# Loading the first tokens' keys and queries in fp32 and reordering the opening of a window-attention and SwiGLU kernel

## The chip, the cores and the metric

The kernel runs on one core of a Trainium2 chip. The metric is device time in microseconds: 252.29 us, the median of three runs (251.28 to 253.04) of the kernel before. The profiled execution took 250.18 us, of which the trace spans 247.8 us. TensorE ran at its full granted clock throughout.

## The reference

The kernel computes attention with a sliding window of 128 tokens plus four "sink" tokens, for 4 sequences of 768 tokens and 8 heads of 64, and feeds the result, seen as 3072 tokens of 512, to a gated feed-forward layer with 1536 hidden units.

```python
scores = scale * np.matmul(q, k.transpose(0, 1, 3, 2))
keep = is_sink | in_window            # key < 4, or 0 <= query - key < 128
scores = np.where(keep, scores, -1e9)
a = np.exp(scores - max); a = a / (sum(a) + 1e-9)
x = (a @ v).transpose(0, 2, 1, 3).reshape(B * S, H * D)
g = x @ w_gate
out = (g * sigmoid(g) * (x @ w_val)) @ w_out
```

## The kernel before

Tokens are handled in 12 groups of 256, three to a sequence. For a group, keys and queries are transposed (`step_T`), multiplied (`step_S`, followed by an exp on ScalarE and a 0/1 mask on VectorE), combined with the values (`step_PV`, followed by a normalisation on VectorE that gives `xn`), and the result is transposed to `xT` (`step_X`). `step_K` does the scores of the four sink keys, which groups after the first of a sequence need apart. The feed-forward part works on blocks of 256 or 512 tokens: `gate` units (gate product `pg`, tanh `th`, value product `pv`, then `u` and `ht` on VectorE), and `down` products. Blocks 0, 1 and 2 are groups 0, 1 and 2. Each engine runs its own instructions in the order in which they are written; the order is laid out by hand.

```python
# loads of the opening: half of group 0's heads by the hardware queues in fp32, half by GpSimd as bf16
for i, eng in ((0, nc.sync), (1, nc.scalar)):
    st = stp.tile([P, 4, 2 * D], FP32, tag="st", name="st")
    eng.dma_start(st, by_two((k, q)[i], 0))
    first.append(st)
nc.scalar.activation(warmed, one, AF.Exp)
nc.gpsimd.dma_start(x0[:, 0, 4:8], by_two(k, 4))
# ... iota tq, iota tk (for identity and masks)
nc.gpsimd.dma_start(x0[:, 1, 4:8], by_two(q, 4))
load_rows(1); load_v(0); load_gate(0); load_v(1)
# ... iota th8 (for the sink table), load_gate(1..3), load_rows(2), load_v(2), load_gate(4), load_out(0..3)
```

```python
def gate(tb, f, attn):
    # ...
    pg = project(wgs, "pg")
    th = tpool.tile([P, 512], FP32, tag="th", name="th")
    nc.scalar.activation(th, pg, AF.Tanh, scale=0.5)
    for a in attn:
        a()                                   # attention steps woven into this unit
    pv = project(wvs, "pv")
    u = upool.tile([P, 512], BF16, tag="u", name="u")
    nc.vector.scalar_tensor_tensor(u, th, 1.0, pg, op0=ALU.add, op1=ALU.mult)
    nc.vector.tensor_tensor(hts[tb][:, f:f + two]..., u, pv, op=ALU.mult)
    flush()                                   # VectorE work put off by the attention steps
```

```python
# the opening
fill(8, ...)                                  # dummy matmuls
for p in range(2):                            # pairs of heads
    nc.vector.tensor_copy(out=x0[:, 0, h], in_=first[0][:, h])
    nc.scalar.copy(out=x0[:, 1, h], in_=first[1][:, h])
    pair_T(p, "a")                            # transposes; key copied by ScalarE, query by VectorE
pair_S(0, 1)                                  # scores and exp of a pair; 1: one dummy matmul first
pair_T(2, "v")
pair_S(1)
pair_mask(0)
pair_T(3, "v"); pair_S(2, 1); pair_mask(1); pair_S(3, 1); pair_mask(2)
step_T(1, 0, 0, "a"); pair_mask(3); step_T(1, 1, 0, "v"); step_T(1, 0, 1, "a"); step_T(1, 1, 1, "v")
step_S(1, 0)                                  # its masks are put off as masks1
step_PV(0, 0, 0); step_PV(0, 0, 1); flush()
step_PV(0, 1, 0); step_PV(0, 1, 1); step_X(0, 0); flush()
step_S(1, 1); step_X(0, 1)
# ... xT of group 0, tables lt8 and diag_h, step_ks(0) (kss and vsb), then the four masks1
us = [g0[0], (alone, 0, 0), g0[1], g1[0], g1[1],
      g0[2], g1[2], g0[3], g1[3], g0[4], g1[4], g0[5], g1[5],
      *g2, *downs(0), *downs(1), *downs(2)]
weave(us, slots((0, [K(1)]), (1, PVs(1) + Xs(1)),
                ((5, 5, 6, 6), T(2)), ((7, 8), Ss(2)), (8, [K(2)]), ...))
```

Of the kernel before, what the change touches and what calls it, by code (L numbers as in the profile page):

```python
# [14 lines left out]
def kernel(  # L15
# [12 lines left out]
    nc = tc.nc  # L28
# [31 lines left out]
    wpool = pool("wpool", 1)  # L60
    rowp = pool("rowp", 3)
    natp = pool("natp", 3)
    stp = pool("stp", 2)
    vpool = pool("vpool", 1)
    kqtp = pool("kqtp", 2)
    epool = pool("epool", 2)
# [101 lines left out]
    def by_two(src, h0):  # L168
        return src[0, h0:h0 + 4, 0:256].rearrange("h (m r) d -> m h (r d)", r=2)

    x0 = const.tile([P, 2, H, 2 * D], BF16)
    first = []
    for i, eng in ((0, nc.sync), (1, nc.scalar)):
        st = stp.tile([P, 4, 2 * D], FP32, tag="st", name="st")
        eng.dma_start(st, by_two((k, q)[i], 0))
        first.append(st)
    nc.scalar.activation(warmed, one, AF.Exp)

    nc.gpsimd.dma_start(x0[:, 0, 4:8], by_two(k, 4))
    nc.gpsimd.iota(tq, [[1, P]], base=0, channel_multiplier=0,  # L180
                   allow_small_or_imprecise_dtypes=True)
    nc.gpsimd.iota(tk, [[0, 1]], base=0, channel_multiplier=1,
                   allow_small_or_imprecise_dtypes=True)
    nc.gpsimd.dma_start(x0[:, 1, 4:8], by_two(q, 4))
    load_rows(1)
    load_v(0)
    load_gate(0)
    load_v(1)
    nc.gpsimd.iota(th8, [[-32, NP2], [-NS, 2]], base=0, channel_multiplier=1,
                   allow_small_or_imprecise_dtypes=True)  # L190
    load_gate(1)
    load_gate(2)
    load_gate(3)
# [63 lines left out]
    def step_ks(b):  # L257
        for h in range(2):
            r = slice(h * D, (h + 1) * D)
            nc.vector.tensor_copy(  # L260
                out=kss[r, b, :, h * NS:(h + 1) * NS], in_=kTs[b][r, :, 0:NS])
        vsb = const.tile([P, H, D + 1], BF16, tag=f"vsb{b}", name="vsb")
        nc.vector.tensor_tensor(  # L263
            vsb,
            vcf[:, b:b + 1].broadcast_to([P, H, D + 1]),
            diag_h.rearrange("q (h o) -> q h o", o=1).broadcast_to([P, H, D + 1]),
            op=ALU.mult)
        vsbs.append(vsb)
# [74 lines left out]
    def dense(t, c, n):  # L343
        return t[:, 0:c * n].rearrange("p (c n) -> p c n", c=c)

    def step_X(g, j):
        t0 = g * 256 + j * P
        tb = max(i for i in range(len(SIZES)) if OFF[i] <= t0)
        off = t0 - OFF[tb]
        if off == 0:  # L350
            xTs[tb] = dense(xtp.tile([P, DMC * 512], BF16, tag="xT", name="xT"),
                            DMC, SIZES[tb])
        if g >= XB:
            def sp():
                nc.sync.dma_start_transpose(xTs[tb][:, :, off:off + P], xns[g, j])
            later.append(sp)
            return
        pt = bank([P, DMC, P], BF16, "px")
        for i in range(DMC):
            nc.tensor.transpose(pt[:, i], xns[g, j][:, i * P:(i + 1) * P], ident)  # L360

        def dve():
            nc.vector.tensor_copy(out=xTs[tb][:, :, off:off + P], in_=pt)  # L363
        later.append(dve)
# [109 lines left out]
    def pair_T(p, key_eng):  # L474
        new_T(0)
        pt = bank([P, 2, 256], FP32, "pt")
        for i in range(2):
            for r in range(2):
                for w in range(2):
                    nc.tensor.matmul(  # L480
                        pt[64 * w:64 * (w + 1), i, r:256:2],
                        x0[:, i, 2 * p + w, r * D:(r + 1) * D], ident,
                        start=True, stop=True, skip_group_check=True)
        if key_eng == "a":
            nc.scalar.copy(out=kTs[0][:, p, 0:256], in_=pt[:, 0])
        else:
            nc.vector.tensor_copy(out=kTs[0][:, p, 0:256], in_=pt[:, 0])
        nc.vector.tensor_copy(out=qTs[0][:, p, 0:256], in_=pt[:, 1])

    def pair_S(p, n=0):  # L490
        if p == 0:
            e_t[0] = epool.tile([P, H, 512], BF16, tag="e", name="e")
        pss = [bank([P, 512], FP32, "s") for _ in range(2)]
        fill(n, pss[0])
        for kk, n, col in ((0, 256, P), (P, P, 3 * P)):
            for h in range(2):
                r = slice(h * D, (h + 1) * D)
                nc.tensor.matmul(
                    pss[h][:, col:col + n], kTs[0][r, p, kk:kk + P],
                    qTs[0][r, p, kk:kk + n], start=True, stop=True)  # L500
        for h in range(2):
            nc.scalar.activation(
                e_t[0][:, 2 * p + h, P:512], pss[h][:, P:512], AF.Exp, scale=scale)

    def pair_mask(p):
        e = e_t[0][:, 2 * p:2 * p + 2, P:512]
        m = mask0.rearrange("q (o a) x -> q o (a x)", o=1)[:, :, P:512]
        nc.vector.tensor_tensor(e, e, m.broadcast_to([P, 2, 384]), op=ALU.mult)

    fill(8, bank([P, 512], FP32, "w"))  # L510
    for p in range(2):
        h = slice(2 * p, 2 * p + 2)
        nc.vector.tensor_copy(out=x0[:, 0, h], in_=first[0][:, h])
        nc.scalar.copy(out=x0[:, 1, h], in_=first[1][:, h])
        pair_T(p, "a")
    pair_S(0, 1)
    pair_T(2, "v")
    pair_S(1)
    pair_mask(0)
    pair_T(3, "v")  # L520
    pair_S(2, 1)
    pair_mask(1)
    pair_S(3, 1)
    pair_mask(2)
    step_T(1, 0, 0, "a")
    pair_mask(3)
    step_T(1, 1, 0, "v")
    step_T(1, 0, 1, "a")
    step_T(1, 1, 1, "v")
    step_S(1, 0)  # L530
    masks1 = list(later)
    later.clear()
    step_PV(0, 0, 0)
    step_PV(0, 0, 1)
    flush()
    step_PV(0, 1, 0)
    step_PV(0, 1, 1)
    step_X(0, 0)
    flush()
    step_S(1, 1)  # L540
    step_X(0, 1)
    masks1 += later[:2]
    del later[:2]
    flush()

    nc.vector.tensor_scalar(lt8, th8, float(NS), None, op0=ALU.is_lt)
    nc.vector.scalar_tensor_tensor(diag_h, th8, 0.0, lt8, op0=ALU.is_ge, op1=ALU.mult)
    step_ks(0)
    for m in masks1:
        m()  # L550
    load_rows(3)
    load_v(3)

    g0, g1, g2 = gates(0), gates(1), gates(2)
    us = [g0[0], (alone, 0, 0), g0[1], g1[0], g1[1],
          g0[2], g1[2], g0[3], g1[3], g0[4], g1[4], g0[5], g1[5],
          *g2, *downs(0), *downs(1), *downs(2)]

    def L(*fs):
        def f():  # L560
            for x in fs:
# [1 line left out]
        return f  # L563

    weave(us, slots(
        (0, [K(1)]), (1, PVs(1) + Xs(1)),
        ((5, 5, 6, 6), T(2)), ((7, 8), Ss(2)), (8, [K(2)]),
        ((9, 9, 10, 10), PVs(2)), (11, Xs(2)),
        (12, [L(A(load_nat, 4), A(load_v, 4), A(load_nat, 5), A(load_v, 5),
                A(load_nat, 6), A(load_v, 6))]),  # L570
        ((13, 14, 15, 16), T(3)), ((17, 18), Ss(3)), (18, [A(step_ks, 1)]),
        (15, [A(xbar, 4)]), (18, [A(xbar, 5)]),
        ((19, 19, 20, 20), PVs(3)), (21, Xs(3)),
        ((20, 21), Ss(4)), (21, [K(4)]),
        ((22, 22, 23, 23), PVs(4)), (23, Xs(4))))

    def pair(ga, gb, sh=0):
        s = sh
# [5 lines left out]

    weave(gates(3) + downs(3), slots(
        (0, [L(A(load_nat, 7), A(load_v, 7))]), (1, [A(xbar, 6)]),
        (2, [L(A(load_nat, 8), A(load_v, 8))]), (5, [A(step_ks, 2)]), *pair(5, 6),
        (6, [A(xbar, 7)]), (7, [L(A(load_nat, 9), A(load_v, 9))]),
        (15, [A(xbar, 8)]), (15, [L(A(load_nat, 10), A(load_v, 10))])))
    weave(gates(4) + downs(4), slots(  # L590
        *pair(7, 8), (3, [A(xbar, 9)]), (9, [A(step_ks, 3)]),
        (3, [L(A(load_nat, 11), A(load_v, 11))]), (15, [A(xbar, 10)])))
    weave(gates(5) + downs(5), slots(*pair(9, 10), (6, [A(xbar, 11)])))
    us = gates(6) + gates(7) + downs(6) + downs(7)
# [38 lines left out]
```

The softmax here doesn't subtract the row's maximum and nothing guards it: scores larger than these inputs give would overflow.

## Time and profile before

| what | value |
|---|---|
| time, median of 3 runs | 252.29 us |
| span of the trace | 247.8 us |
| TensorE matmul busy | 236.3 us (95%) |
| VectorE busy | 165.2 us (67%) |
| ScalarE busy | 109.4 us (44%) |
| moved by DMA | 27.35 MB, mean 110 GB/s |
| chain that ended last | PE 85%, DVE 10%, ACT 3%, issue 1% |

In the profile PE is TensorE's matmuls and PEld its weight loads, DVE is VectorE, ACT is ScalarE, POOL is GpSimd and SP is SyncE. A timeline row gives the start in us, the duration in us, engine, source line, operation, what is written from what, and how many instructions were merged into the row; in brackets stands the idle time before it and what ended it. A row of the waits gives who waited for whom, the total in us, how often, and the longest. In the slices each digit is a fortieth of the span, in tenths of busy time. Short names in the rows: `e` are the exponentials, `xn` the normalised attention result, `px` its transpose in PSUM, `pt` transposed keys or queries in PSUM, `x` the bf16 keys and queries of group 0.

### The profile page before, as it was taken

The numbers are of one execution on the slowest core, as the hardware profiler recorded it, in microseconds if no ns is written. First come the engines' busy times: TensorE is split into PE (matmuls) and PEld (weight loads), VectorE is DVE, ScalarE is ACT, GpSimd is POOL, SyncE is SP. The second block draws the span as 40 slices with busy tenths as digits, with TensorE's granted clock in tenths as the row PEclk, the third lists the DMA queues.
The fourth block names the chain that finished last, engine by engine and source line by source line (L and its number), as shares of the span: only waits on it lengthen the run. The fifth ranks groups of instructions, "written<-read, shape, count | busy, mean of one in ns | idle before, by whom it ended". The sixth has DMA issues, their size and how long they took to land.

```text
span 247.8 us, 5063 instructions
## 1 busy us (share of the span) xinstructions
PE 236.3 (95%) x2007; PEld 135.9 (55%) x2007; DVE 165.2 (67%) x347; ACT 109.4 (44%) x213; POOL 69.3 (28%) x91
## 2 busy tenths in 40 slices
PE   7885999999999999999999999999999999999994
PEld 2554887787655445444445455445454445478443
DVE  5799669877965189993198993198981289887100
ACT  3780348133655383631474721465611662333112
POOL 8965824993672008070043000000000000000000
PEclk9999999999999999999999999999999999999999
DMA  8999999999999759997569802551103200100132
GB/s 140 161 185 196 190 206 199 158 152 128 156 181 189 172 128 86 134 120 104 152 122 139 58 15 67 154 140 24 42 3 115 97 0 3 42 3 0 42 127 85
DMA packets 100390, 27.35 MB, mean 110 GB/s; under 512 B 86416, under 2 KB 97424, under 8 KB 100368
## 3 DMA queue, kind: packets, MB, share of 16 engines
q0 software_dynamic: 69440, 13.90, 74.7%
q1 hardware_dynamic: 30400, 12.89, 22.5%
q8 instruction: 15, 0.25, 0.4%
q10 hardware_dynamic: 528, 0.26, 0.4%
q14 instruction: 7, 0.06, 0.1%
HBM read 28.34 MB, written 6.29 MB: 140 GB/s over the span
## 4 chain that ended last, share of the span: by engine, by line
PE 85%; DVE 10%; ACT 3%; issue 1%; DVEq 0%
PE pd L414 25%; PE pv L383 24%; PE pg L383 22%; PE o L331 4%; PE s L285 4%; DVE ht L397 3%; DVE xn L337 2%; PE pt L239 2%; DVE e L297 1%; PE w L471 1%; ACT e L292 1%; DVE u L396 1%; PE pt L480 1%; PE px L360 1%; DVE vsb L263 1%
## 5 line engine op out<-in xcount | busy, mean ns | idle before, releaser
L390 ACT ACTIVATE th<-pg 128x512 f32<-128x512 f32 x72 | 43.5, 604 | 75.4 <-PE pg L383 73.3
L383 PE MATMUL pv<-xT,wv 128*128 128x256 bf16 (+1 forms) x384 | 74.3, 326 | 0.7 <-DVE ht L397 0.7
L383 PE MATMUL pg<-xT,wg 128*128 128x256 bf16 (+1 forms) x384 | 74.2, 326 | 0.6 <-DVE xT L363 0.5
L396 DVE SCALAR_TENSOR_TENSOR u<-th,pg 128x512 bf16<-128x512 f32 x72 | 49.2, 683 | 34.6 <-ACT th L390 34.3
L414 PE MATMUL pd<-wo,ht 128*128 128x512 bf16 (+1 forms) x300 | 66.0, 371 | 0.0
L397 DVE TENSOR_TENSOR ht<-u,pv 128x512 bf16<-128x512 bf16 x72 | 49.5, 688 | 10.7 <-PE pv L383 4.5
L383 PEld LDWEIGHTS <-wg 128*128 128x128 bf16 x384 | 37.5, 98 | 25.9 <-issue 0.6
L383 PEld LDWEIGHTS <-wv 128*128 128x128 bf16 x384 | 34.2, 97 | 20.7 <-issue 2.5
L292 ACT ACTIVATE e<-s 128x512 bf16<-128x512 f32 (+1 forms) x88 | 42.9, 581 | 3.6 <-PE s L285 3.5
L414 PEld LDWEIGHTS <-ht 128*128 128x128 bf16 x300 | 28.0, 98 | 28.6 <-issue 0.3
L418 ACT ACTIVATE ot<-pd 128x512 f32<-128x512 f32 (+1 forms) x25 | 14.6, 583 | 50.9 <-PE pd L414 50.9
L297 DVE TENSOR_TENSOR e<-e,mask 128x1024 bf16<-128x1024 bf16 (+1 forms) x44 | 26.8, 649 | 2.9 <-ACT e L292 2.9
L111 POOL DMA_DIRECT2D nat<-in_k_dram x16 | 14.1, 898 | 44.7 <-DMA qT<-nat 33.7
L122 POOL DMA_DIRECT2D va<-in_v_dram x24 | 21.5, 916 | 7.0 <-DMA nat<-in_q_dram 3.5
L337 DVE TENSOR_TENSOR xn<-o,rcp 128x256 bf16<-128x256 f32 x48 | 20.4, 425 | 1.7
L331 PEld LDWEIGHTS <-e 128*128 128x128 bf16 x352 | 16.6, 98 | 6.8 <-DVE e L297 0.6
L331 PE MATMUL o<-va,e 128*128 128x65 bf16 x352 | 18.2, 193 | 0.4 <-DVE e L297 0.3
L111 POOL DMA_DIRECT2D nat<-in_q_dram x16 | 14.3, 910 | 2.4 <-DMA nat<-in_k_dram 2.4
L336 DVE RECIPROCAL rcp<-o 128x4 f32<-128x4 f32 x48 | 8.5, 177 | 7.1 <-PE o L331 7.0
L285 PE MATMUL s<-qT,kT 64*128 64x128 bf16 (+1 forms) x240 | 12.9, 237 | 0.2 <-DVE qT L246 0.2
L285 PEld LDWEIGHTS <-kT 64*128 64x128 bf16 x240 | 7.8, 94 | 7.2 <-issue 6.6
L331 PE MATMUL o<-vsb,es 128*128 128x260 bf16 x32 | 8.8, 274 | 0.3 <-ACT es L311 0.3
(57 smaller groups left out, 92.2 us busy)
## 6 DMA issues: line engine op xcount, KB each, us to landing
out_dram<-ot SPq DMA_DIRECT2D x23, 256.0 KB
va<-in_v_dram POOLq DMA_DIRECT2D x24, 128.0 KB, 7.7
nat<-in_k_dram POOLq DMA_DIRECT2D x16, 128.0 KB, 6.6
nat<-in_q_dram POOLq DMA_DIRECT2D x16, 128.0 KB, 7.8
wo<-in_moe_w_out_dram POOLq DMA_DIRECT2D x4, 384.0 KB, 11.9
wg<-in_moe_w_gate_dram POOLq DMA_DIRECT2D x4, 256.0 KB, 8.2
wv<-in_moe_w_val_dram POOLq DMA_DIRECT2D x4, 256.0 KB, 8.8
rows<-in_k_dram POOLq DMA_DIRECT2D x6, 128.0 KB, 9.1
```

The lines of the kernel that those rows point to most:

```text
L111: nc.gpsimd.dma_start(x[:, i, j].rearrange("p (h d) -> p h d", d=D), src[b, :, t0:t0 + P].rearrange("h p d -> p h d"))
L122: nc.gpsimd.dma_start(va[:, j, :, 0:D], v[b, :, t0:t0 + P].rearrange("h p d -> p h d"))
L285: nc.tensor.matmul(pss[2 * pp + h][:, col:col + n], kTs[b][r, p, kk:kk + P], qTs[b][r, p, qq:qq + n], start=True, stop=True)
L292: nc.scalar.activation(e_t[g][:, h0 + h, lo:512], pss[2 * pp + h][:, lo:512], AF.Exp, scale=scale)
L297: nc.vector.tensor_tensor(e, e, m[:, :, lo:512].broadcast_to([P, 2, 512 - lo]), op=ALU.mult)
L331: nc.tensor.matmul(o, l, r, start=(i == 0), stop=(i == len(mms) - 1), skip_group_check=True)
L337: nc.vector.tensor_tensor(xns[g, j][:, 256 * hh:256 * (hh + 1)].rearrange("p (h d) -> p h d", h=4), po[:, :, 0:D], rcp.broadcast_to([P, 4, ...
L383: nc.tensor.matmul(ps[:, i * n:(i + 1) * n], ws[fi][:, c, fo * P:(fo + 1) * P], x[:, c], start=(c == 0), stop=(c == DMC - 1))
L390: nc.scalar.activation(th, pg, AF.Tanh, scale=0.5)
L396: nc.vector.scalar_tensor_tensor(u, th, 1.0, pg, op0=ALU.add, op1=ALU.mult)
L397: nc.vector.tensor_tensor(hts[tb][:, f:f + two].rearrange("p a n -> p (a n)"), u, pv, op=ALU.mult)
L414: nc.tensor.matmul(po, hts[tb][:, f, ts * P:(ts + 1) * P], wos[f // n][:, f % n, lo:hi], start=(f == 0), stop=(f == DFC - 1))
```

## The change

All of group 0's keys and queries now come in fp32 by the hardware queues of SyncE and ScalarE, in four pieces, and are cast to bf16 by VectorE (keys) and ScalarE (queries); GpSimd is left free to issue the loads of group 1 at once. The casts stand ahead of the transposes that need them, the small tables for the sink keys are made early, and the dummy matmuls between the scores are gone. ScalarE takes over the query transposes of group 1 and the `xT` copies of group 1. The transposes of group 1 are split around the value products of group 0. The value products of group 1 stood together after the first gate unit; they are now in two parts with a gate unit between them, and a third gate unit of block 0 holds the `xT` step of group 1. The aim is that TensorE has gate work while VectorE normalises. The sink value table (`vsb`) is a step of its own, so that it can be placed apart.

```diff
-    stp = pool("stp", 2)
...
-    for i, eng in ((0, nc.sync), (1, nc.scalar)):
-        st = stp.tile([P, 4, 2 * D], FP32, tag="st", name="st")
-        eng.dma_start(st, by_two((k, q)[i], 0))
-        first.append(st)
+    st = [rowp.tile([P, H, 2 * D], FP32, tag="rows", name="st") for _ in range(2)]
+    for h in range(0, H, 4):
+        for i, eng in ((0, nc.sync), (1, nc.scalar)):
+            eng.dma_start(st[i][:, h:h + 4], by_two((k, q)[i], h))
...
-    nc.gpsimd.dma_start(x0[:, 0, 4:8], by_two(k, 4))
...
-    nc.gpsimd.dma_start(x0[:, 1, 4:8], by_two(q, 4))
     load_rows(1)
+    nc.gpsimd.iota(th8, ...)                  # moved up from after load_v(1)
...
-    def step_X(g, j):
+    def step_X(g, j, evict="v"):
...
+        if evict == "a":
+            nc.scalar.copy(out=xTs[tb][:, :, off:off + P], in_=pt)
+            return
...
+    def cast(i, p):                           # i 0: keys, on VectorE; 1: queries, on ScalarE
...
-    def pair_S(p, n=0):
+    def pair_S(p):
-        fill(n, pss[0])
...
-    for p in range(2):
-        ...
-        pair_T(p, "a")
-    pair_S(0, 1)
-    ...
+    for i, p in ((0, 0), (1, 0), (0, 1), (1, 1)):
+        cast(i, p)
+    pair_T(0)
+    cast(0, 2)
+    cast(1, 2)
+    pair_T(1)
+    cast(0, 3)
+    cast(1, 3)
+    pair_S(0)
+    pair_T(2)
+    pair_S(1)
+    pair_T(3)
+    nc.vector.tensor_scalar(lt8, th8, float(NS), None, op0=ALU.is_lt)
+    nc.vector.scalar_tensor_tensor(diag_h, th8, 0.0, lt8, op0=ALU.is_ge, op1=ALU.mult)
     pair_mask(0)
+    pair_S(2)
+    step_ks(0)
     pair_mask(1)
+    pair_S(3)
     pair_mask(2)
     step_T(1, 0, 0, "a")
+    step_T(1, 1, 0, "a")
     pair_mask(3)
+    step_PV(0, 0, 0)
+    step_PV(0, 0, 1)
+    flush()
     step_T(1, 0, 1, "a")
+    step_T(1, 1, 1, "a")
+    step_PV(0, 1, 0)
+    step_PV(0, 1, 1)
+    flush()
     step_S(1, 0)
     masks1 = list(later)
     later.clear()
+    step_X(0, 0)
+    step_X(0, 1)
     flush()
+    step_K(1)
+    step_vsb(0)
+    step_S(1, 1)
+    later[:0] = masks1
+    flush()
...
-    us = [g0[0], (alone, 0, 0), g0[1], g1[0], g1[1],
-          g0[2], g1[2], g0[3], g1[3], g0[4], g1[4], g0[5], g1[5],
+    us = [g0[0], (alone, 0, 0), g0[1], (alone, 0, 0), g0[2], g1[0], g1[1],
+          g1[2], g0[3], g1[3], g0[4], g1[4], g0[5], g1[5],
...
-        (0, [K(1)]), (1, PVs(1) + Xs(1)),
-        ((5, 5, 6, 6), T(2)), ((7, 8), Ss(2)), (8, [K(2)]),
+        (1, PVs(1)[:2]), (3, PVs(1)[2:]),
+        (4, [A(step_X, 1, 0, "a"), A(step_X, 1, 1, "a")]),
+        ((6, 6, 7, 7), T(2)), ((8, 9), Ss(2)), (9, [K(2)]),
```

More of the change, by code (lines that the diff above doesn't have):

```diff
@@ L171 @@
     x0 = const.tile([P, 2, H, 2 * D], BF16)
-    first = []
-    for i, eng in ((0, nc.sync), (1, nc.scalar)):
-        st = stp.tile([P, 4, 2 * D], FP32, tag="st", name="st")
-        eng.dma_start(st, by_two((k, q)[i], 0))
-        first.append(st)
+    st = [rowp.tile([P, H, 2 * D], FP32, tag="rows", name="st") for _ in range(2)]
+    for h in range(0, H, 4):
+        for i, eng in ((0, nc.sync), (1, nc.scalar)):
+            eng.dma_start(st[i][:, h:h + 4], by_two((k, q)[i], h))
     nc.scalar.activation(warmed, one, AF.Exp)
-    nc.gpsimd.dma_start(x0[:, 0, 4:8], by_two(k, 4))
     nc.gpsimd.iota(tq, [[1, P]], base=0, channel_multiplier=0,
@@ L183 @@
                    allow_small_or_imprecise_dtypes=True)
-    nc.gpsimd.dma_start(x0[:, 1, 4:8], by_two(q, 4))
     load_rows(1)
+    nc.gpsimd.iota(th8, [[-32, NP2], [-NS, 2]], base=0, channel_multiplier=1,
+                   allow_small_or_imprecise_dtypes=True)
     load_v(0)
@@ L188 @@
     load_v(1)
-    nc.gpsimd.iota(th8, [[-32, NP2], [-NS, 2]], base=0, channel_multiplier=1,
-                   allow_small_or_imprecise_dtypes=True)
     load_gate(1)
@@ L261, in step_ks, with step_vsb @@
                 out=kss[r, b, :, h * NS:(h + 1) * NS], in_=kTs[b][r, :, 0:NS])
+    def step_vsb(b):
         vsb = const.tile([P, H, D + 1], BF16, tag=f"vsb{b}", name="vsb")
@@ L472, in fill, with pair_T @@
                              skip_group_check=True)
-    def pair_T(p, key_eng):
+    def cast(i, p):
+        h = slice(2 * p, 2 * p + 2)
+        if i == 0:
+            nc.vector.tensor_copy(out=x0[:, i, h], in_=st[i][:, h])
+        else:
+            nc.scalar.copy(out=x0[:, i, h], in_=st[i][:, h])
+    def pair_T(p):
         new_T(0)
@@ L483, in pair_T @@
                         start=True, stop=True, skip_group_check=True)
-        if key_eng == "a":
+        if p < 2:
             nc.scalar.copy(out=kTs[0][:, p, 0:256], in_=pt[:, 0])
@@ L510 @@
     fill(8, bank([P, 512], FP32, "w"))
-    for p in range(2):
-        h = slice(2 * p, 2 * p + 2)
-        nc.vector.tensor_copy(out=x0[:, 0, h], in_=first[0][:, h])
-        nc.scalar.copy(out=x0[:, 1, h], in_=first[1][:, h])
-        pair_T(p, "a")
-    pair_S(0, 1)
-    pair_T(2, "v")
+    for i, p in ((0, 0), (1, 0), (0, 1), (1, 1)):
[8 more added lines that the diff above has]
+    pair_T(2)
     pair_S(1)
+    pair_T(3)
+    nc.vector.tensor_scalar(lt8, th8, float(NS), None, op0=ALU.is_lt)
+    nc.vector.scalar_tensor_tensor(diag_h, th8, 0.0, lt8, op0=ALU.is_ge, op1=ALU.mult)
     pair_mask(0)
-    pair_T(3, "v")
-    pair_S(2, 1)
+    pair_S(2)
+    step_ks(0)
     pair_mask(1)
-    pair_S(3, 1)
+    pair_S(3)
     pair_mask(2)
     step_T(1, 0, 0, "a")
+    step_T(1, 1, 0, "a")
     pair_mask(3)
-    step_T(1, 1, 0, "v")
+    step_PV(0, 0, 0)
+    step_PV(0, 0, 1)
+    flush()
     step_T(1, 0, 1, "a")
-    step_T(1, 1, 1, "v")
+    step_T(1, 1, 1, "a")
+    step_PV(0, 1, 0)
+    step_PV(0, 1, 1)
+    flush()
     step_S(1, 0)
@@ L532 @@
     later.clear()
-    step_PV(0, 0, 0)
-    step_PV(0, 0, 1)
+    step_X(0, 0)
+    step_X(0, 1)
     flush()
-    step_PV(0, 1, 0)
-    step_PV(0, 1, 1)
-    step_X(0, 0)
+    step_K(1)
+    step_vsb(0)
+    step_S(1, 1)
+    later[:0] = masks1
     flush()
[L540 to L550, printed above, removed]
     load_rows(3)
@@ L565 @@
     weave(us, slots(
-        (0, [K(1)]), (1, PVs(1) + Xs(1)),
-        ((5, 5, 6, 6), T(2)), ((7, 8), Ss(2)), (8, [K(2)]),
-        ((9, 9, 10, 10), PVs(2)), (11, Xs(2)),
-        (12, [L(A(load_nat, 4), A(load_v, 4), A(load_nat, 5), A(load_v, 5),
-                A(load_nat, 6), A(load_v, 6))]),
[L571 to L575, printed above, removed]
+        (1, PVs(1)[:2]), (3, PVs(1)[2:]),
+        (4, [A(step_X, 1, 0, "a"), A(step_X, 1, 1, "a")]),
+        ((6, 6, 7, 7), T(2)), ((8, 9), Ss(2)), (9, [K(2)]),
+        ((10, 10, 11, 11), PVs(2)), (12, Xs(2)),
+        (13, [L(A(load_nat, 4), A(load_v, 4), A(load_nat, 5), A(load_v, 5),
+                A(load_nat, 6), A(load_v, 6))]),
+        ((14, 15, 16, 17), T(3)), ((18, 19), Ss(3)), (19, [A(step_ks, 1)]),
+        (19, [A(step_vsb, 1)]),
+        (16, [A(xbar, 4)]), (19, [A(xbar, 5)]),
+        ((20, 20, 21, 21), PVs(3)), (22, Xs(3)),
+        ((21, 22), Ss(4)), (22, [K(4)]),
+        ((23, 23, 24, 24), PVs(4)), (24, Xs(4))))
     def pair(ga, gb, sh=0):
@@ L586 @@
         (0, [L(A(load_nat, 7), A(load_v, 7))]), (1, [A(xbar, 6)]),
-        (2, [L(A(load_nat, 8), A(load_v, 8))]), (5, [A(step_ks, 2)]), *pair(5, 6),
+        (2, [L(A(load_nat, 8), A(load_v, 8))]), (5, [A(step_ks, 2), A(step_vsb, 2)]), *pair(5, 6),
         (6, [A(xbar, 7)]), (7, [L(A(load_nat, 9), A(load_v, 9))]),
@@ L590 @@
     weave(gates(4) + downs(4), slots(
-        *pair(7, 8), (3, [A(xbar, 9)]), (9, [A(step_ks, 3)]),
+        *pair(7, 8), (3, [A(xbar, 9)]), (9, [A(step_ks, 3), A(step_vsb, 3)]),
         (3, [L(A(load_nat, 11), A(load_v, 11))]), (15, [A(xbar, 10)])))
```

## The prediction

> **What bounds the kernel now.** I read the page's busy line and its 40 slices first, to see which engine is full and where it is not.
>
> ```profile
> PE 236.3 (95%) x2007; PEld 135.9 (55%) x2007; DVE 165.2 (67%) x347; ACT 109.4 (44%) x213; POOL 69.3 (28%) x91
> ...
> PE   7885999999999999999999999999999999999994
> ...
> DVE  5799669877965189993198993198981289887100
> ACT  3780348133655383631474721465611662333112
> ```
>
> TensorE is full in every slice except the first four (6.2 us each) and the last. So only the first 25 us can give much: whatever comes later merely starts sooner. The busy time of each engine in the stages of that opening is next (PE, PEld, DVE, ACT, POOL, clock, DMA share, GB/s).
>
> ```profile
> 5.00:10.00 5.00, 3.80 (x47) 1.96 (x43) 2.48 (x7) 2.75 (x7) 5.00 (x8) 1.00 1.52 156
> 10.00:15.00 5.00, 4.33 (x109) 3.44 (x107) 4.27 (x11) 4.33 (x10) 4.55 (x7) 1.00 1.83 170
> 15.00:20.00 5.00, 4.20 (x54) 2.98 (x54) 4.80 (x15) 3.48 (x8) 2.70 (x5) 1.00 1.57 193
> 20.00:25.00 5.00, 2.43 (x40) 1.74 (x37) 4.71 (x15) 0.00 (x0) 3.13 (x4) 1.00 1.45 196
> ```
>
> From 20 to 25 us TensorE is idle half the time and ScalarE does nothing, while VectorE is full. The timeline says why:
>
> ```profile
> 18.26 2.49 DVE L297 TENSOR_TENSOR e<-e,mask 128x1024 bf16<-128x1024 bf16 x4
> ...
> 21.46 0.69 DVE L397 TENSOR_TENSOR ht<-u,pv 128x512 bf16<-128x512 bf16 x1
> ...
> 23.92 0.42 DVE L337 TENSOR_TENSOR xn<-o,rcp 128x256 bf16<-128x256 f32 x1
> ...
> 24.26 0.89 DVE L363 COPY xT<-px 128x512 bf16<-128x512 bf16 x2
> ...
> 24.52 1.04 PE L383 MATMUL pg<-xT,wg 128*128 128x256 bf16 x8
> ...
> 25.60 0.60 ACT L390 ACTIVATE th<-pg 128x512 f32<-128x512 f32 x1 [6.57 <-PE pg L383]
> ```
>
> After block 0's first gate unit, group 1's four value products wait for VectorE's masks, normalisations and two xT copies. The queue behind them, all gate work, starts at 24.5. The waits of 5 to 30 us give sizes:
>
> ```profile
> ACT th L390 <- PE pg L383: 9.1, 4, 6.6
> ...
> DVE qT L488 <- ACT kT L485: 2.5, 2, 1.4
> ...
> PE px L360 <- DVE xn L337: 2.4, 3, 1.3
> ...
> PE pt L480 <- DVE x L513: 1.2, 1, 1.2
> ```
>
> [...]
>
> **The change part by part.** I choose as yardstick P, the start of the fifth gate unit (of 256 tokens), which is also the first that carries transposes of group 2. Before, four units precede it; after, again four (block 0 units 0, 1, 2 and block 1 unit 0, where it was two of each). What follows P is the same sequence with one unit of block 0 in the place of one of block 1, so the gain at P is the gain at the end. Before, the chain of waits puts P at 29.93 us. I now lay out the new order by hand, with durations from the trace.
>
> *Loads.* Keys and queries become four fp32 pieces of 256 KB. The first two were used at 4.24 and 4.59 us. The trace shows up to 340 GB/s between 3 and 4 us, so 0.52 MB more take about 1.6 us, and some more in company of the software queue: landed at about 6.3 (an estimate from these two numbers). The bf16 halves left about the same DMA work (0.26 MB at 150 GB/s is 1.7 us), so later loads arrive much as before. GpSimd, before each issue from 14 us on, waited for the transfer eight places earlier to land, about 1.35 us apart; read through these waits the second weight pair landed at 18.7 and 20.0, the third at 21.3 and 22.7. Gate unit 1 and 2 of block 0 may not start sooner.
>
> *Front of group 0.* Added: two casts on VectorE and two on ScalarE, 0.36 to 0.41 us each. Removed: three filler matmuls of 0.39. ScalarE: casts to 5.3, first kT 5.6 to 6.0, cast at 6.3 to 6.75, second kT to 7.15, last cast, then eight exps at 0.43 apart to about 11. VectorE, at 0.42 each: qT to 6.4, cast 6.8, qT 7.6, cast 8.0, then kT, qT, kT, qT to 9.7; the two small sink tables 0.3 more, the four masks 4 x 0.55, kss 0.3: the last mask ends at 12.5. Before it ended at 12.41. The opening of group 0 gains nothing at this point, though its scores are some 0.6 us earlier, as the casts and tables went ahead of the masks.
>
> *Group 1.* TensorE: the value product behind the last mask 12.5 to 12.75, transposes 1.1 us, then two value products to 14.35, scores of the first half of the heads to 14.9 (before 13.68). ScalarE now evicts all four transposes (4 x 0.6) and exponentiates from 14.65: 4 x 0.52 to 16.7, the sink exps 0.38 to 17.1, 4 x 0.52 to 19.15, first tanh to 19.75. VectorE lost two qT evictions of 0.65 but its own chain is no longer alone: four normalisations (0.55 each) to 15.25, two xT 0.89 to 16.15, vsb 0.70 to 16.85, two masks to 18.1; the third waits for exps at 18.1, the fourth ends at 19.15 + 0.6 = 19.75, before 20.75. **Gain here: 1.0 us.**
>
> *Gate units between.* TensorE: unit 0 at 16.75 to 18.5 (before 17.09), two value products to 19.2, unit 1 to 20.95 (its second weights at 20.0 just about), two more to 21.65, gate half of unit 2 to 22.5. VectorE from 19.75: u and ht 1.4 to 21.15, two normalisations 1.1 to 22.25, u and ht to 23.6, two normalisations to 24.7. Then the transposes of xn 0.3, value half of unit 2 0.87, to 25.9; ScalarE copies xT meanwhile (2 x 0.6, from 24.5 to 25.7). Block 1 unit 0 is 1.75: **P at 27.65 instead of 29.93, 2.3 us sooner.**
>
> The arithmetic in short: xn of group 1 is finished at 24.7, 0.35 us later than before (24.35), because 1.0 us of earlier masks is less than the extra u and ht of unit 1 (1.37). But of the four gate units two and a half lie ahead of it, where there was one: 1.5 x 1.75 = 2.6. So 2.6 - 0.3 = 2.3. Time: 252.29 - 2.3 = 250.0.
>
> **The rivals.** (a) DMA becomes the bound: gate units 1 and 2 move into the time in which their weights land (20.0 and 22.7). For it: DMA share is over 1.4 throughout. Against: unit 2's value half isn't needed before 25 in my layout, so there is 2 us of slack. If VectorE were much faster than I think, P would be at best 22.7 + 0.87 + 1.75 = 25.3, a gain of 4.6: time 247.7. That is also a ceiling, 1.8%. (b) The second fp32 halves land late and stand in front of kT on ScalarE, whose queue is in order: each us beyond 6.3 pushes the last mask, the scores of group 1 and everything after by nearly as much. At 8 us the gain falls to 0.7: 251.6. For it: two queues and the software queue share the engines, with the DMA share at 1.7 from 4 to 5 us. Against: nothing else is in the hardware rings but eight 4 KB loads. (c) ScalarE as the new bound: it gets 0.8 us of casts, 1.3 of evictions and 1.2 of xT. In 20 to 25 us it had 5 us to spare, but in 10 to 15 it was already at 4.33, so group 1's exps may slip by 1 us; the gain would be 1.3, 251.0. (d) The gain is given back later: from 36 to 48 us the old chain already ran through ScalarE exps and VectorE normalisations (TensorE busy 4.65 and 4.47 of 5), and block 0's and 1's backlog may add a few tenths.
>
> **Range and chances.** (b), (c) and (d) pull toward 251.5, (a) bounds the other side at 247.7, and the three runs before spread over 1.8 us. I take 250.0, and 248.3 to 251.5 for eight in ten. Over 2% faster would need 247.2, beyond the ceiling: 0.04. Over 2% slower would need the new order to stall somewhere I don't see, 5 us: 0.03. Within 2%: 0.93.
>
> **What would show it.** In the new profile: the second fp32 halves cast at 6.3 to 8 us; the last group-0 mask at 12.5; the last group-1 mask at 19.75; TensorE busy more than 4 of 5 us between 20 and 25 (2.43 now); xn of group 1 ready at 24.7; P at 27.65; and the later stages the same length. The reading is wrong if the last group-0 mask is over 1 us off, if gate units wait on weights, or if the gain at 30 us isn't the gain at the end.

## The result, and the profile after

The changed kernel takes 248.77 us (median of 4, 248.25 to 249.13) against 252.09 us of the kernel before in the same comparison: a ratio of 0.9865, with a 95% interval of 0.9824 to 0.9906. A second comparison gave 0.9922 (0.9891 to 0.9953; the medians were 249.05 and 251.28 us). The prediction was 250.0 us with a range of 248.3 to 251.5.

The two traces that can be laid side by side differ by less: the spans are 247.8 and 246.7 us. Single executions scatter, those of the kernel before from 249.6 to 255 us and ten of the changed one from 248.2 to 249.4, so below I compare lowest times and traces where a part of the span is at stake, and ratios for the whole. The ratios leave out executions that lie over 1.5% above the fastest of the same kernel; medians and ranges do not. Most traces come from the low end of their kernel's times; where one does not, the text says so.

The busy lines and slices of the changed kernel's page:

```profile
PE 235.0 (95%) x1981; PEld 136.5 (55%) x2004; DVE 163.7 (66%) x345; ACT 111.7 (45%) x219; POOL 67.8 (27%) x89
...
PE   7796999999999999999999999999999999999994
...
DVE  5988378876955199992298993198980389887100
ACT  4893347234654473621564721555611662333112
PEclk9999799999999999999999999999999999999999
```

In TensorE's row one of the thin slices of the opening, the third (12 to 19 us), has become a full one; the fourth is still at 6. The row of the clock is new: in the fifth slice it stands at 7. It was 9 (full) throughout before. Then the stages of the opening, with the columns as before (PE, PEld, DVE, ACT, POOL, clock, DMA share, GB/s):

```profile
5.00:10.00 5.00, 3.90 (x68) 2.40 (x66) 3.94 (x14) 4.47 (x14) 4.95 (x8) 1.00 1.70 200
10.00:15.00 5.00, 4.28 (x100) 3.19 (x94) 4.22 (x14) 3.55 (x9) 3.70 (x5) 1.00 1.82 183
15.00:20.00 5.00, 5.00 (x70) 4.38 (x67) 4.54 (x9) 4.32 (x10) 2.47 (x5) 1.00 1.46 194
20.00:25.00 5.00, 2.66 (x39) 2.17 (x38) 4.29 (x12) 1.42 (x3) 3.37 (x5) 1.00 1.45 196
25.00:30.00 5.00, 5.00 (x38) 3.70 (x37) 2.06 (x3) 1.02 (x3) 4.15 (x6) 0.66 1.69 189
```

From 15 to 20 us TensorE works without a break. From 20 to 25 it still stands half the time, and from 25 to 30 it is always busy with only 38 matmuls, at two thirds of its clock. The timeline shows both:

```profile
18.26 0.69 DVE L295 TENSOR_TENSOR e<-e,mask 128x1024 bf16<-128x1024 bf16 x1 [0.29 <-ACT e L290]
...
19.67 0.69 DVE L399 TENSOR_TENSOR ht<-u,pv 128x512 bf16<-128x512 bf16 x1
...
20.52 1.04 PE L385 MATMUL pg<-xT,wg 128*128 128x256 bf16 x8
...
23.86 0.40 PE L358 MATMUL px<-ident,xn 128*128 128x128 bf16 x4 [2.19 <-DVE xn L335]
...
23.92 0.42 DVE L335 TENSOR_TENSOR xn<-o,rcp 128x256 bf16<-128x256 f32 x1
...
24.18 1.13 ACT L361 COPY xT<-px 128x512 bf16<-128x512 bf16 x2 [1.99 <-PE px L358]
...
25.62 1.91 PE L385 MATMUL pg<-xT,wg 128*128 128x256 bf16 x8
```

The last mask of group 1 ends at 18.95 (20.75 before). The last `xn` of group 1 is written at 24.34, exactly as before, because `u` and `ht` of a second gate unit stand ahead of it; but by then TensorE has done two and a half gate units instead of one. A gate half (eight matmuls of 256 columns) that took 1.04 us takes 1.91 at 25.6. The chain of waits around the start of the fifth gate unit, my yardstick P, first P in the kernel before, then the changed kernel:

```profile
29.93 0.87 PE pg L383 x8
```

```profile
24.69 1.14 PE pv L385 x8
25.83 1.71 PE pg L385 x8
27.54 1.44 PE pv L385 x8
28.98 0.87 PE pg L385 x8
```

P is at 28.98 (29.93 before): 0.95 us sooner. The three halves before it took 4.29 us where 3 x 0.87 = 2.61 is usual, so the clock took 1.68 us; without that P is at 27.3, 2.6 us sooner.

### The profile page after: what moved, and what is told of

The parts are those of the page before. It is cut to its first block, busy times and chain, and to the rows that moved or that the text cites. A ratio compares the mean times of both kernels' runs of the same rounds, so it can differ in the third digit from the quotient of the medians.

```text
span 246.7 us, 5043 instructions
## 1 busy us (share of the span) xinstructions
PE 235.0 (95%) x1981; PEld 136.5 (55%) x2004; DVE 163.7 (66%) x345; ACT 111.7 (45%) x219; POOL 67.8 (27%) x89
## 4 chain that ended last, share of the span: by engine, by line
PE 84%; DVE 9%; ACT 4%; issue 1%; DVEq 0%
PE pd L416 25%; PE pv L385 24%; PE pg L385 22%; PE o L329 4%; PE s L283 3%; ACT e L290 3%; DVE ht L399 3%; PE pt L235 2%; DVE xn L335 2%; DVE u L398 1%; PE w L473 1%; DVE e L516 1%; PE pt L489 1%; DVE e L295 1%; ACT th L392 0%
## 5 line engine op out<-in xcount | busy, mean ns | idle before, releaser
L416 PE MATMUL pd<-wo,ht 128*128 128x512 bf16 (+1 forms) x291 | 65.0, 370 | 0.6 <-issue 0.2
L385 PEld LDWEIGHTS <-wv 128*128 128x128 bf16 x384 | 34.7, 99 | 21.2 <-issue 2.8
```

Of the source, the lines that this page charges most:

```text
L385: nc.tensor.matmul(ps[:, i * n:(i + 1) * n], ws[fi][:, c, fo * P:(fo + 1) * P], x[:, c], start=(c == 0), stop=(c == DMC - 1))
L416: nc.tensor.matmul(po, hts[tb][:, f, ts * P:(ts + 1) * P], wos[f // n][:, f % n, lo:hi], start=(f == 0), stop=(f == DFC - 1))
```

## The experiments

**The same two kernels again**, to see what is the order and what the execution.

> The kernel before once more, to see the span and granted clock of every execution. The trace of the kernel before had a full clock and took 250.18 us, but its timed runs 251.3 to 253.0; that of the changed kernel 249.06. If the clock explains the difference (theory: the changed order is worth 1.7 to 2.3 us, and the remainder of the measured 3.3 is a clock that falls more often in the old order), several of these executions show a mean clock below 1.00 and spans 1 to 3 us over 247.8, and those at a clock of 1.00 stay within 0.3 us of 247.8. Rival: the order alone is worth 3.3 us; then all spans lie at 249 to 250 with the clock at 1.00 and the profiled one was a lucky draw.

> The changed kernel once more, for a tight ratio. Theory: 0.985 to 0.992. The execution traced first had the TensorE clock at half between 25 and 29 us, at a loss of 1.7 us there; if that is a draw of the execution, some executions here are at 246.0 to 246.1 with a clock of 1.00, and some at 246.7. Rival: the fall of the clock belongs to the new order (an idle TensorE from 21.7 to 23.9 and then full load); then nearly every execution has it, at the same place.

The kernel before: median 252.28 us, and a trace that is the first one over again (249.61 us, span 247.8, clock 1.00, P at 29.89). The spans and mean clocks of its 22 executions bear out the theory. The four with a mean clock of 1.00 have spans of 247.7 to 247.9 us; the other 18 have 0.98 to 0.993 and spans of 249.4 to 251.8 us. The rival, with the clock at 1.00 in all, is out. The clock does not explain every difference: of 57 more executions of this kernel, 11 at a mean clock of 1.00 have spans of 249.1 to 249.3 us. No trace of a longer execution was had, so where the clock falls in one of them is not known.

The changed kernel: 248.24 to 249.38 us; its trace has the clock at half again, now from 24.1 to 27.6 us, and P at 28.97. Together with the first comparison, six of its ten executions have a mean clock of 0.992 or 0.993 and spans of 246.7 to 246.9 us, four have 0.998 or 1.00 and 246.0 or 246.1 us. So the fall of the clock is a frequent draw of the execution, not a fixed part of the new order, and costs 0.6 to 0.9 us at the end.

**Each half of the change alone.** First the split without the new opening:

```diff
-    us = [g0[0], (alone, 0, 0), g0[1], g1[0], g1[1], g0[2], g1[2], ...
+    us = [g0[0], (alone, 0, 0), g0[1], (alone, 0, 0), g0[2], g1[0], g1[1], g1[2], ...
-        (0, [K(1)]), (1, PVs(1) + Xs(1)),
+        (0, [K(1)]), (1, PVs(1)[:2]), (3, PVs(1)[2:]),
+        (4, [A(step_X, 1, 0, "a"), A(step_X, 1, 1, "a")]),
```

> The kernel before with only the second half of the change: the values of group 1 in two parts around the second gate unit of block 0, the transposes of group 1 in the third with copies by ScalarE; loads and opening as before. Theory (the split is the gain): xn of group 1 is ready 1.4 us later than in the kernel before, at 25.7, but two and a half gate units lie ahead of it instead of one: P at about 28.7 instead of 29.9, time 1.0 to 1.5 us under before. Rival (the opening is the gain): 0 to 0.4 us under before.

The changed kernel with the old weave is the other half (the two lists above, the other way round).

> The changed kernel with the old weave: the loads, casts and opening are new, but group 1's four value products stand together behind the first gate unit, with the transposes and VectorE's xT copies in the same place. Theory (the split is the gain): the last mask of group 1 comes at 19.0 instead of 20.75, so everything behind it moves by up to 1.7 us: P at 28.2 to 28.5, time 1.0 to 1.7 us under before, as much as the split alone and half of both. Rival (the opening gives nothing that lasts): the time of before.

The split alone: `xn` ready at 25.77, P at 28.72, 1.2 us sooner than before, as the theory has it; yet the ratio is 0.997 (0.9946 to 0.9994) and the lowest time 249.54, the same as the kernel before's 249.6. The gain at P was there and did not reach the end. (The median is 1.2 us lower, 250.08 against 251.28, with a mean clock of 0.998 or more in 14 of 20 executions against 20 of 57.) The opening alone: the last mask of group 1 at 18.95, P at 29.33 with a clock fall on the way (its two halves from 23.0 took 2.83 instead of 1.74 us; without it 28.2), the ratio 0.9926 (0.9907 to 0.9945), the lowest time 247.96. The clock fell in 20 of its 22 executions (mean 0.993 or less); at a clock of 0.999 or 1.00 its span is 246.1 us, the changed kernel's too. So the opening carries the gain in time, and the split adds to P but little to the end. Where that goes shows the trace of the split alone, in the waits from 75 to 90 us (first, from the timeline of the kernel before, the gate half that there starts without a wait):

```profile
85.00 1.02 PE L383 MATMUL pg<-xT,wg 128*128 128x512 bf16 x4
```

```profile
PEld L387 <- DMA xT<-xn: 2.8, 1, 2.8
...
PE pg L387 <- DMA xT<-xn: 2.3, 1, 2.3
```

The first gate half of block 3 waits for `xT` of group 4, which goes by two DMA transposes from group 4 on (in the kernel, `XB = 4`), where earlier groups are transposed by TensorE. In the kernel before, that wait was 0.5 us of the weight load and nothing of the matmul. The trace of the split is of one of its longest executions (252.85 us), so the 2.3 us are more than is usual for it; the lowest times alone say that some 1.2 us, the gain at P, are lost on the way.

**Filling TensorE's standstill** in the changed kernel:

```diff
-        (4, [A(step_X, 1, 0, "a"), A(step_X, 1, 1, "a")]),
+        (4, [lambda: fill(10, bank([P, 512], FP32, "w")),
+             A(step_X, 1, 0, "a"), A(step_X, 1, 1, "a")]),
```

> The changed kernel with ten dummy matmuls (128x512, 0.22 us each at full clock) between the gate half of the third unit and the transposes of group 1, so that TensorE does not stand still while it waits there. The wait is 2.2 us, so nothing is delayed. Two of two traces of the changed kernel show the TensorE clock at half for about 3.6 us right after this wait. Theory (a standstill of about 2 us followed by full load brings the fall): with the wait filled the clock stays at 1.00 to 30 us, the fifth gate unit starts at 27.3 instead of 28.97, and the time falls by 0.5 to 1.7 us under the changed kernel. Rival (the fall comes by itself some 20 us into the program): it is there again at 24 to 29 us, and the time is that of the changed kernel.

The clock stayed up in all six executions (means of 0.998 to 1.00, against six falls in ten before), so the rival of a fall that comes by itself is out. The stages of the trace:

```profile
20.00:25.00 5.00, 4.82 (x49) 3.14 (x47) 4.35 (x12) 1.27 (x3) 3.11 (x4) 1.00 1.45 195
25.00:30.00 5.00, 5.00 (x70) 4.32 (x68) 2.77 (x6) 2.21 (x4) 4.41 (x7) 1.00 1.68 189
```

From 25 to 30 us 70 matmuls ran instead of 38. P was at 27.46, 1.5 us before that of the changed kernel; the time fell to a median of 248.25 (248.05 to 248.82), only some 0.7 us lower. The missing 0.8 us is at block 3 again: its first matmul, at 83.36, had a wait for the DMA transposes ahead of it.

```profile
83.36 1.02 PE L385 MATMUL pg<-xT,wg 128*128 128x512 bf16 x4 [0.87 <-DMA xT<-xn]
```

**Two orders with a sooner P.** All four value products behind the first gate unit (`(1, PVs(1))`, no second stop, transposes in the third unit), and one more unit of block 0 before the transposes (`g0[2], g0[3], g1[0]`, transposes at place 5):

> The changed kernel with group 1's four value products together behind the first gate unit, so that VectorE normalises all of them before u and ht of the second unit; gate unit 2 follows, and the transposes with ScalarE's copies stay in the third unit. Theory (VectorE's order sets when xn of group 1 is ready): xn is ready at 23.0 instead of 24.35, the value half of the third unit starts at 23.0 to 23.3 instead of 24.7, the wait of TensorE before it shrinks from 2.2 to under 1 us, and the fifth gate unit starts at 25.6 to 25.9 at full clock: 1.4 us under the changed kernel in an execution without a fall of the clock. Rival (the split of the values as the change has it is the best order): 0.5 to 1.5 us over the changed kernel.

> The changed kernel with one more unit of block 0 ahead of group 1's transposes, which stand in the fourth unit; block 1 begins after it. Theory (TensorE's 2.2 us of waiting is filled by the value half of unit 2 and the gate half of unit 3, whose weights land at 22.7 and 24.1): the fifth unit starts at 26.3 to 26.6 instead of 27.3, 0.7 to 1.0 us under the changed kernel in an execution without a fall of the clock. Rival (the weights of unit 3 land too late, or the time is set later): no gain, within 0.3 us of the changed kernel.

Both reach the fifth unit about as expected or sooner, at 25.93 and 25.69 us. (The 25.05 us that a later expectation gives for the first is misread: it is the value half of the fourth unit, and the lead over the changed kernel at full clock is 1.4 us, not 2.4.) Neither is better in time: lowest 248.18 and 248.22, as in the changed kernel (248.24), ratios 0.992 (0.9879 to 0.9961) and 0.9964 (0.9928 to 1.0), medians over all executions 252.19 and 250.27. Their shortest spans are 245.9 us each, as good as the changed kernel's 246.0, so the sooner P is lost even there. Block 3 is where it goes. First the changed kernel's DMA transposes as SyncE issued them and the first gate half that needs them, then the same two in the trace with the values together, which is of a long execution (252.73 us):

```profile
79.65 2.50 SPq L353 DMA_TRANSPOSE xT<-xn  x2
```

```profile
83.84 1.03 PE L385 MATMUL pg<-xT,wg 128*128 128x512 bf16 x4
```

```profile
76.59 3.27 SPq L353 DMA_TRANSPOSE xT<-xn  x2
```

```profile
84.94 1.44 PE L385 MATMUL pg<-xT,wg 128*128 128x512 bf16 x3 [3.99 <-DMA xT<-xn]
```

Issued at 76.6, landed at about 84.9; in the changed kernel issued at 79.65 and there in time for 83.84. Three us sooner in, no sooner out. The other order, whose trace is of a middling execution (250.26 us), shows the same: issued at 76.46, and the gate half starts at 83.84 after a wait of 3.0 us. What the landing does follow in the traces is GpSimd's loads of groups 7 and 8 (`nat`, `va`), issued between 60 and 77 us, whose waits (0.3 to 3.1 us each in these traces) ended with other transfers and never with TensorE. From the end of their last issue (74.4, 74.6, 75.2 and 76.9 us with the standstill filled, the later transposes, the values together and the split alone) to the gate half that had waited for the transposes (83.36, 83.84, 84.94 and 86.05) it is 9.0 to 9.8 us, while from the issue of the transposes it is anything from 5.2 to 8.4. That fits transposes held up by these loads; no run changed the loads alone at this place. In the other order the clock fell right after the wait:

```profile
84.00:86.00 2.00, 2.00 (x17) 0.81 (x16) 0.47 (x1) 1.10 (x3) 0.00 (x0) 0.76 0.86 219
86.00:88.00 2.00, 2.00 (x6) 0.76 (x5) 0.70 (x2) 1.46 (x3) 0.00 (x0) 0.50 0.49 109
```

**Group 4 transposed by TensorE**, which takes the DMA transposes off that path:

```diff
-    XB = 4
+    XB = 5
```

> The kernel before with group 4's result transposed by TensorE and copied by VectorE, as groups 0 to 3 are, instead of by the two DMA transposes that block 3 waits for at 83 to 86 us. The executions of the kernel before lie in clusters at 249.6, 251.3, 252.3 and 253.6; its two traces, both from the quick end, show that wait at 0 to 0.5 us. Theory (the wait for the DMA transposes, with the fall of the clock after it, makes the slower clusters): most executions come within 0.5 us of 249.5 and the median falls from 251.4 by 1.5 us or more. Rival (the clusters come from elsewhere): the same clusters, median within 0.4 us.

> The changed kernel with group 4's result transposed by TensorE. Theory (the gain of 2.5 us that the new opening has at its fifth gate unit is cut by a wait of 0.9 us for the DMA transposes at 83 us, when the clock stays up): 0.3 to 0.9 us under the changed kernel in an execution without a fall of the clock at 25 us, no change in one with it; median 248.0 to 248.8. Rival (the wait is covered anyway): within 0.2 us of 248.9, or a few tenths slower by the 0.9 us of added VectorE copies.

> The order with all of group 1's values behind the first gate unit, and group 4's result transposed by TensorE. Without the latter it had the fifth gate unit at 25.05 us, 2.4 us ahead of the changed kernel at full clock, and then stood 4.0 us at block 3 for the DMA transposes, which were issued 3.1 us sooner and landed no sooner than in the changed kernel. Theory (the loads of groups 7 and 8 fill the DMA engines until some 83 us, and this alone gives the opening's gain back): the wait is gone and the time is 245.0 to 246.5. Rival (something else at the same place holds it, or a fall of the clock follows any gain): 247.5 or more.

In the kernel before the time stays (ratio 1.0016, 0.999 to 1.0042; the lowest is 0.7 us higher), and clusters with a lowered mean clock are still there, so those do not come from that wait: the rival stands for them. One cluster is gone: of the executions at a mean clock of 0.998 or more, all 8 have spans of 248.5 or 248.6 us, where 5 of 11 of the kernel before in the same comparison stand at 249.1 or more. In the changed kernel the trace has P at 27.30 with the clock at 1.00, block 3 begins at 82.61 without a wait, and the span is 245.8; the ratio is 0.9912 (0.9883 to 0.9941), the lowest 247.95 against 248.24, the median 249.24. So the wait is gone, for 0.3 us at the lowest times, and the median, for which I had set 248.0 to 248.8, does not show even that: the transposes on TensorE cost something too (0.8 us in the kernel before, spans 248.6 against 247.8), and the clock fell in 11 of 22 executions (mean 0.993 or less). With the values together the gain shows fully:

```profile
15.00:20.00 5.00, 4.45 (x73) 3.75 (x73) 4.52 (x10) 3.86 (x9) 2.61 (x5) 1.00 1.46 194
20.00:25.00 5.00, 4.83 (x48) 4.09 (x46) 4.65 (x13) 2.16 (x4) 3.14 (x4) 1.00 1.45 196
...
80.00:85.00 5.00, 5.00 (x34) 2.27 (x33) 1.81 (x3) 3.23 (x7) 0.00 (x0) 1.00 1.13 220
```

No standstill between 20 and 25, none between 80 and 85, no fall of the clock: 246.81 us (246.53 to 247.34, six executions), ratio 0.9835 (0.9791 to 0.9878), span 244.5. This beats both kernels. It missed my upper mark of 246.5 by 0.3.

The three traces with group 4 on TensorE, all at full clock, settle where the gain at P had gone. P in the kernel before, the changed kernel and the order with the values together:

```profile
30.04 0.87 PE pg L383 x8
```

```profile
27.30 0.87 PE pg L385 x8
```

```profile
25.98 0.87 PE pg L385 x8
```

P comes 2.7 and another 1.3 us sooner; the spans are 248.6, 245.8 and 244.5 us, 2.8 and another 1.3 shorter. With these DMA transposes out of the way the whole gain at P reaches the end. With them, 2.6 us at P (27.3 against 29.93) had become 1.7 to 1.8 at full clock, and the further 1.4 to 1.6 us of the two sooner orders nothing.

**The loads alone**, in the kernel before: `st` in four fp32 pieces, the two GpSimd loads gone, and each pair's casts just ahead of its transposes; then the same with `fill(10, ...)` instead of `fill(8, ...)` at the start.

> The kernel before with group 0's keys and queries all in fp32 by the hardware queues, cast just ahead of the transposes that need them; the rest as before. Theory (the loads only make room and gain nothing alone): VectorE and ScalarE get 0.8 us of casts each, the last mask of group 0 ends at 12.4 to 13.0 (12.41 before), and the time is within 0.6 us of the kernel before. Rival (the loads are the gain): masks 0.7 us earlier and the time 1 us lower.

> The loads alone (4.2 us slower than the kernel before), with ten dummy matmuls at the start instead of eight, so that TensorE has no pause of 0.26 us before the first transposes. There, eight transposes took 1.06 us and eight 64x128 score and row transposes ran at 0.6 of the speed that the same shapes have in the kernel before (0.63 us for eight), though the granted clock reads 1.00. [...] Rival (the casts' place in the queues is what costs 4 us): the transposes stay at 1.06 or the time stays within 1 us of 255.5.

The loads alone are 1.7% slower (ratio 1.0172, 1.0106 to 1.0239; median 255.55 us). That was in neither theory. The timeline of TensorE shows it; here are the dummy matmuls at the start and the first two pairs' transposes:

```profile
1.23 3.60 PE L467 MATMUL w<-zero 128*128 128x512 bf16 x8 [1.23 <-DVE zero L160]
5.08 1.06 PE L476 MATMUL pt<-ident,x 128*64 128x128 bf16 x8 [0.26 <-DVE x L509]
7.45 1.06 PE L476 MATMUL pt<-ident,x 128*64 128x128 bf16 x8 [1.31 <-DVE x L509]
```

And with two more dummy matmuls:

```profile
1.23 4.40 PE L467 MATMUL w<-zero 128*128 128x512 bf16 x10 [1.23 <-DVE zero L160]
5.55 0.63 PE L476 MATMUL pt<-ident,x 128*64 128x128 bf16 x8
7.45 0.63 PE L476 MATMUL pt<-ident,x 128*64 128x128 bf16 x8 [1.27 <-DVE x L509]
```

The same transposes, 1.06 against 0.63 us, and the difference ahead of them is two more dummies in the place of a pause of 0.26 us. The median falls to 253.77 (ratio 1.0104, 1.0069 to 1.014), the last mask of group 0 from 16.27 to 14.56 us. So the slower rate explains about 1.8 of the 4.2 us, if most executions have it as the one trace does (the lowest times, 253.74 and 252.97, differ by 0.8 only); I had expected more of it, a last mask by 13.8 and a time of 253.0 at most. The other 2.3 us stay without the pause; in this order each later pair's transposes wait for their cast (0.66 and 0.85 us for the last two), which the changed kernel avoids by casting ahead. How much of the 2.3 that is was not measured by itself.

## Why the prediction was right, point by point

**The bound.** Right: the opening, 20 to 25 us, where VectorE was busy 4.71 of 5 us and TensorE 2.43. What the change did there is less than I wrote. I said that TensorE would be busy more than 4 of 5 us; it is 2.66. My own layout did not give the 4 us: it leaves TensorE idle from 22.5 to 24.7, 2.2 us, and 2.19 was measured. The work that fills the standstill came from a place further left: 15 to 20 us are full (5.00, 4.20 before) and the standstill lies at 21.7 to 23.9. I had placed the gate units some 1.1 us too late and let unit 1 end at 20.95 instead of about 19.8.

**The loads.** The second fp32 halves were cast at 6.25 and 6.30 us (predicted 6.3). Wrong was that later loads would arrive much as before. The pair of rows from the timelines, the kernel before and then the changed one, is the gate load that must wait for an earlier gate load to land:

```profile
14.38 0.74 POOL L132 DMA_DIRECT2D wg<-in_moe_w_gate_dram  x1 [0.45 <-DMA wg<-in_moe_w_gate_dram]
```

```profile
12.93 0.74 POOL L131 DMA_DIRECT2D wg<-in_moe_w_gate_dram  x1 [0.54 <-DMA wg<-in_moe_w_gate_dram]
```

The stream on the software queue came 1.45 us sooner at this place. It did no harm to the estimate, as no gate unit waited for weights either way. That the two added fp32 pieces give the DMA engines about as much work as the two bf16 halves did was my estimate, which no run measured by itself; a share of 1.70 from 5 to 10 us, 1.52 before, only shows the engines busy. My conclusion from it, that later loads would gain nothing, was wrong: group 1's rows were issued 1.9 us sooner (1.37 instead of 3.29 us), and the stream behind them kept 1.45 of it. That may be more than a side effect. With the old loads the split alone gets no lower than a span of 247.4 us, with the new opening every order without group 4 on TensorE stops at 245.8 to 246.1; the difference is about the 1.45 us. Which part of the opening gives the gain at the end, the sooner loads or the sooner masks, was not separated.

**Front of group 0.** The last mask at 11.68 instead of 12.5 (before 12.41): mis-sized by 0.8. I had the eight exps 0.43 us apart; they took 3.30 in all and none held up a mask, and the VectorE copies, 0.41 or 0.42 us each, overlapped more than I allowed: those of a pair's keys and queries started 0.34 us apart (7.54 and 7.88, 8.38 and 8.72). The layout has the query copies of pairs 0 and 1 on VectorE start behind ScalarE's key copies. So it was measured, at 5.96 (after a wait of 0.78) and 6.96 us with the key copies ended at 5.92 and 6.94; no run had these copies in another order.

**Group 1.** The last mask at 18.95 instead of 19.75, the same 0.8 us carried on. Its step was right: sooner by 1.8 us rather than 1.0.

**Gate units between.** The arithmetic was that `xn` comes later by the second unit's `u` and `ht` less the gain of the masks, while one and a half more units lie ahead of it. Measured: `xn` at 24.34, not later at all (predicted 24.7), and 2.6 us gained at P at full clock (predicted 2.3). Right in mechanism and nearly in size.

**"The gain at P is the gain at the end."** This is the step that failed, although the total came out. In the first trace P was 0.95 us sooner for a clock at half, which no part of the prediction had; and when the clock is up, of 2.6 us only 1.7 to 1.8 arrive (spans 247.8 against 246.0 and 246.1), because block 3 waits for DMA transposes whose landing does not move with TensorE (0.87 us in the trace with the standstill filled, which has the same P within 0.2 us). This is the third of the signs that I had named for a wrong reading. Rival (d), giving back later, was the right kind of rival at the wrong place: I looked at 36 to 48 us, and it was 83 us.

**The other rivals.** (a) Weights did not bind. (b) The halves were in time. (c) ScalarE's exps did order group 1: the last mask waited 0.29 us for one, and no more.

**The time.** 250.0 against 248.77. By the spans the order is worth 1.1 us where its own clock falls and 1.7 to 1.8 where neither kernel's does; the comparisons gave 3.3 and 2.2 in the medians. The rest is mostly the granted clock of the kernel before: 18 of 22 and 37 of 57 of its executions have a mean of 0.993 or less, and the step from 1.00 to 0.993 lengthens most of their spans from 247.8 us to between 249.4 and 249.6, where it lengthens the changed kernel's, in six of ten executions, from 246.0 us to between 246.7 and 246.9. So the number came out in part by luck: less of the gain at P reached the end than I said, and falls of the clock that I knew nothing of, dearer in the kernel before, made up for it. Open stay what decides in which execution the clock falls, and why spans differ at one mean clock (247.8 and 249.1 at 1.00, 249.4 and 251.9 at 0.993).

## What to carry to other kernels

A gain measured early in a kernel is a gain only if everything that later work waits for moves with it. The DMA transposes of group 4 did not: issued at 76.59 us instead of 79.65 with the values together, they held the gate half until 84.94 and became the next wait, 3.99 us. So follow the gained time to the end of the trace before adding more of it. When one engine sets a stage, ask in which order it serves two customers: here VectorE's normalisations ahead of the second unit's products were worth more than splitting them around it (P at 25.9 against 27.3). And change loads, casts and their places in the engines' queues together: the loads alone, without the new places for the casts, cost 4 us.

## What the runs showed of the hardware

In seven of the fourteen traces the column of TensorE's granted clock stood at 0.50 for a time: for 3.4 us in six of them, and for 6.8 us, 83.5 to 90.3, with the values together. In the changed kernel it was from about 25.15 to 28.57 us:

```profile
25.00:26.00 1.00, 1.00 (x8) 0.77 (x6) 0.13 (x1) 0.31 (x1) 1.00 (x2) 0.58 1.95 170
26.00:27.00 1.00, 1.00 (x7) 0.70 (x5) 0.56 (x1) 0.00 (x0) 1.00 (x2) 0.50 2.36 166
27.00:28.00 1.00, 1.00 (x7) 0.69 (x6) 0.00 (x0) 0.42 (x1) 0.89 (x2) 0.50 1.62 192
28.00:29.00 1.00, 1.00 (x8) 0.80 (x7) 0.69 (x1) 0.17 (x1) 0.72 (x2) 0.72 1.25 209
```

My estimate from these lengths: 3.4 us at half take 1.7 us of clock from a span of 247, so the mean clock of an execution would read 0.993, with two such falls 0.986, with three 0.979. Most means of the kernel before do lie at 1.00, 0.993, 0.986 and 0.98. So they seem to count the falls also where there is no trace.

In the seven traces with a fall it came within or up to 1.3 us after a stretch in which TensorE stood for 0.8 to 4 us (20 to 26 us, or 81 to 86 us where it waited for DMA there). It did not follow every such stretch: five traces (the kernel before twice and with group 4 on TensorE, the changed kernel with group 4 on TensorE, the loads alone) had a standstill in the opening and a full clock. The mean clocks of the executions make the case stronger. With the 2.2 us of standstill it is 0.993 or less in 6 of 10 executions (11 of 22 with group 4 on TensorE); with the standstill filled, in 0 of 6. The order with the values together, which has no such standstill in the opening, has it in 14 of 16 with the wait at block 3 and in 0 of 6 without that wait. So in these orders the falls go with a standstill of TensorE. Why they follow one in some executions and not in others is not shown.

One slow stretch does not appear in the clock column. In the loads alone, after 3.60 us of dummy matmuls and a pause of 0.26 us, eight transposes took 1.06 us, and the slower rate lasted until 17.7 us, while the mean clock of that trace reads 1.00; with 4.40 us of dummy matmuls and no pause, eight took 0.63 us. One trace each shows the two rates; whether this is the same fall of the clock, left out of the column, or something else is not shown.
